# Decode attention: weights loaded first and used as moving operands, the first pair of chunks inside TensorE's loop, VectorE and ScalarE in rolled loops

## The chip, the cores and the metric

The kernel runs on one core of a Trainium2 chip. The metric is the device time of one execution in microseconds (us). The kernel before takes 665.26 us (median of 4 runs beside the changed kernel, 665.17 to 665.36). Profiles come from one execution each. They start at the first instruction, end about 2 us short of the measured time (663.3 of 665.2 us in the kernel before), and need not fall on the median run; where that matters, the text says so. All times inside an execution are counted from the span's start.

Names of engines: TensorE (PE in the profile; PEld is its weight load), VectorE (DVE), ScalarE (ACT), GpSimd (POOL), and the sync engine (SP), whose sequencer issues nearly all DMAs.

## The reference, cut to what matters

```python
x = A_x                                   # 1 x 1 x 512
xn = _layernorm(x)
# A: 32 query heads on 8 groups of cached keys and values, 65536 keys of 128 each
q = (xn @ wq)                             # 512 x 4096
scores = q k^T * 128 ** -0.5; p = softmax(scores); o = p v
a = o @ wo                                # 4096 x 512
# B: a small feed-forward block
h = gelu(xn @ w1 + b1)                    # 512 x 1792
b = h @ w2 + b2                           # 1792 x 512
return x + a + b
```

The keys and values are 2 x 134 MB, the weights 12 MB more. All must be read once; the arithmetic per byte is small.

## The kernel before

The cache is cut into 32 chunks of 16384 keys, four to a group: K0 to K31 and V0 to V31, 4 MB each. Two chunks make a pair. There are four 4 MB slots in SBUF: two for keys (0 and 1), two for values (2 and 3). At the start, wq lies in slot 2 and w1 with w2 in slot 3. The sync engine issues the chunks in one fixed order, each as soon as its slot is free:

```python
chunks = [("K", 0), ("K", 1)]
for u in range(2, NU):
    chunks += [("K", u), ("V", u - 2)]
...
after_chunk[("K", 0)] = [dma_small, dma_wq]     # x, biases; then wq
after_chunk[("K", 1)] = [dma_w12]
```

A pair transposes each key tile on TensorE (VectorE and ScalarE copy the transposes out of PSUM), multiplies them with q, takes the softmax's maximum and exponentials, and multiplies the values of the pair before. A key slot is free when all of its chunk is transposed (`done_chunk("K", ...)`), so K4 can be asked for only when K2 is transposed, in pair 1.

```python
def pair(i):
    ua, ub = 2 * i, 2 * i + 1
    first = i == 0
    ...
    transposes(0, 3)
    done_chunk("K", ua)
    if first:
        layernorm()
        qproj()              # 128 matmuls, wq stationary, one column each
        load_q(ua)
        scores(0, 0)
    ...
    scores(0, 3)
    v_block(ua - 2, 2)       # nothing when first
    v_block(ua - 2, 3)
    ...
    if first:
        ffn2()
    ...
```

Pair 0 stands in front of TensorE's loop, which then runs 15 turns for pairs 1 to 15. VectorE and ScalarE are unrolled altogether:

```python
@block.scalar
def _(e):
    _emit(e, ACT.ops)
@block.vector
def _(e):
    _emit(e, DVE.ops)
@block.tensor
def _(e):
    folded, growth = _fold([PE.ops[a:b] for a, b in zip(marks, marks[1:])])
    _emit(e, PE.ops[:marks[0]])               # pair 0
    _emit_loop(e, folded, growth, len(marks) - 1)
    _emit(e, PE.ops[marks[-1]:])
```

Of the kernel before, what the change touches and what calls it, by code (L numbers as in the profile page):

```python
# [22 lines left out]
class _Eng:  # L23
    def __init__(self, name, sem, is_pe=False):
        self.name = name
        self.sem = sem
        self.count = 0
        self.clock = {}
        self.ops = []
        self.is_pe = is_pe  # L30
        self.deferred = []

# [11 lines left out]
class _Sched:  # L44


    def __init__(self, nc):
        self.nc = nc
        self.engs = {}
        self.last_write = {}  # L50
        self.reads = {}
        self.dsem_vals = {}

# [52 lines left out]
    def op(self, eng, fn, reads=(), writes=(), publish=True, inc=1):  # L106
        req = self._required(reads, writes)
# [16 lines left out]
        eng.ops.append((waits, fn, pub))  # L124
        return ev

    def wait_ev(self, eng, ev):
        if not eng.knows(ev):
            eng.absorb(ev)
            eng.ops.append(([(ev.sem, ev.val)], None, None))  # L130

    def dma(self, eng, fn, sem, reads=(), writes=(), total=None):
# [14 lines left out]
        eng.ops.append((waits, fn, (sem, 16)))  # L147
# [3 lines left out]
def _fold(bodies):  # L151
# [5 lines left out]
    for i, b in enumerate(bodies):  # L157
        for k, (waits, _, _) in enumerate(b):
            for s, v in waits:
                seen.setdefault((k, s), {})[i] = v  # L160
# [5 lines left out]
    for k in range(len(bodies[0])):  # L166
        assert len({(b[k][2] or (None, 0))[1] for b in bodies}) == 1
        need = {}
        for (kk, s), at in seen.items():
            if kk == k:  # L170
                need[s] = max(v - i * growth[s] for i, v in at.items())
        ops.append((bodies[0][k][1], bodies[0][k][2], need))
    out = []
    known = {}
    for fn, pub, need in ops:
        waits = [(s, v) for s, v in need.items() if known.get(s) is None or known[s] < v]
        for s, v in waits:
            known[s] = v
        out.append((waits, fn, pub))
# [3 lines left out]
def _emit(eng_obj, ops):  # L183
    for waits, fn, pub in ops:
# [9 lines left out]
def _emit_loop(eng_obj, ops, growth, n):  # L194

    uses = {}
    for waits, _, _ in ops:
        for s, v in waits:
            uses.setdefault(s, []).append(v)
    regs, steps = {}, []  # L200
    at = {}
    for s, vs in uses.items():
        key = (vs[0], growth[s]) if len(vs) == 1 else s
        if key not in regs:
            r = eng_obj.alloc_register(f"w{len(regs)}")
            eng_obj.reg_mov(r, vs[0])
            regs[key] = r
            steps.append((r, vs[0] + growth[s] - vs[-1]))
        at[s] = [regs[key], vs[0]]
    with eng_obj.Fori(0, n):  # L210
        for waits, fn, pub in ops:
            for s, v in waits:
                r, now = at[s]
                if v != now:
                    eng_obj.reg_add(r, r, v - now)
                    at[s][1] = v
# [4 lines left out]
        for r, step in steps:  # L221
            eng_obj.reg_add(r, r, step)


def bass_parallel_sum__gqa_block_cached__dense_activation_gelu__decode_kernel(
# [74 lines left out]
    fin_bf = nc.alloc_sbuf_tensor("fin_bf", [128, 128], BF)  # L300

# [21 lines left out]
    negm = nc.alloc_sbuf_tensor("negm", [128, NU * HPG], F32)  # L323
    sums = nc.alloc_sbuf_tensor("sums", [128, NU * HPG], F32)
    o_all = nc.alloc_sbuf_tensor("o_all", [128, NU * HPG], F32)
    nmin = nc.alloc_sbuf_tensor("nmin", [128, H], F32)
    coef = nc.alloc_sbuf_tensor("coef", [128, NU * HPG], F32)
    wtot = nc.alloc_sbuf_tensor("wtot", [128, NU * HPG], F32)
    rden = nc.alloc_sbuf_tensor("rden", [128, H], F32)
    o_c = nc.alloc_sbuf_tensor("o_c", [128, NU * HPG], F32)  # L330
    o_sum = nc.alloc_sbuf_tensor("o_sum", [128, H], F32)
# [32 lines left out]
    for t, res in ((wo_cur, "wo_cur"), (oT_next, "oT_next"), (sums_cur, "sums_cur")):  # L364
# [15 lines left out]
    chunks = [("K", 0), ("K", 1)]  # L380
    for u in range(2, NU):
# [36 lines left out]
    def dma_small():  # L418
        for dst, src, res in (
# [5 lines left out]
            sch.dma(SP, lambda dst=dst, src=src: sp.dma_start(out=dst, in_=src), sem_misc,  # L425
# [33 lines left out]
    after_chunk[("K", 0)] = [dma_small, dma_wq]  # L459
    after_chunk[("K", 1)] = [dma_w12]  # L460
# [71 lines left out]

    def load_q(u):
        g = u // CPG
        sch.op(DVE, lambda g=g: dve.tensor_copy(out=q_cur[:, :], in_=qT_bf[:, g * HPG:(g + 1) * HPG]),
               reads=["qT"], writes=["q_cur"])
# [11 lines left out]
    def stats_2(u):  # L548
        k, us = u % 2, slice(u * HPG, (u + 1) * HPG)
# [5 lines left out]
               reads=["pA"], writes=[f"negm{u}"])  # L555
        src = pss[k][:, 0:CW].rearrange("p (t j) -> p t j", j=HPG)
        for j in range(HPG):
            sch.op(
                ACT,
                lambda k=k, u=u, j=j, src=src: act.activation(  # L560
                    out=P_v[k][:, :, j], in_=src[:, :, j], func=ACTF.Exp,
                    bias=negm[:, u * HPG + j:u * HPG + j + 1], scale=1.0,
                    accum_out=sums[:, u * HPG + j:u * HPG + j + 1]),
                reads=[f"negm{u}", f"pss{k}"],
                writes=[f"P{k}_{j}", f"sums{u}_{j}"],
# [15 lines left out]
    def keep_o(u):  # L581
        us = slice(u * HPG, (u + 1) * HPG)
        sch.op(DVE, lambda us=us: dve.tensor_copy(out=o_all[:, us], in_=pO[:, 0:HPG]),  # L583
               reads=["pO"], writes=[f"o{u}"])


    def qproj():
        for h in range(H):
            for kt in range(KT):
                sch.op(  # L590
                    PE,
                    lambda h=h, kt=kt: pe.matmul(  # L592
                        pA[:, PA_Q + h:PA_Q + h + 1], lhsT=wq_sb[:, kt, h * DH:(h + 1) * DH],
                        rhs=xnT_bf[:, kt:kt + 1], start=kt == 0, stop=kt == KT - 1),
                    reads=[f"slot{NK}", "xnT"], writes=["pA"],
                    publish=h == H - 1 and kt == KT - 1,
                )
        sch.op(DVE, lambda: dve.tensor_scalar(out=qT_bf[:, :], in0=pA[:, PA_Q:PA_Q + H], scalar1=SCALE,
                                              scalar2=None, op0=ALU.mult), reads=["pA"], writes=["qT"])
        slot_free[NK] = True  # L600

    def ffn1():
        for fc in range(FC):
            for kt in range(KT):
                sch.op(
                    PE,
                    lambda fc=fc, kt=kt: pe.matmul(  # L607
                        pA[:, PA_H + fc:PA_H + fc + 1], lhsT=w1_sb[:, kt, fc:F:FC],
                        rhs=xnT_bf[:, kt:kt + 1], start=kt == 0, stop=kt == KT - 1),
                    reads=[f"slot{NK + 1}", "w1", "xnT"], writes=["pA"],  # L610
                    publish=fc == FC - 1 and kt == KT - 1,
                )
# [15 lines left out]
    def ffn2():  # L628
        for kt in range(KT):
            cols = slice(kt * 128, (kt + 1) * 128)  # L630
            for fc in range(FC):
                sch.op(
                    PE,
                    lambda kt=kt, fc=fc, cols=cols: pe.matmul(  # L634
                        pA[:, PA_FT + kt:PA_FT + kt + 1], lhsT=w2_sb[:, fc, cols],
                        rhs=gT_bf[:, fc:fc + 1], start=fc == 0, stop=False),
                    reads=[f"slot{NK + 1}", "w2", "gT"], writes=["pA"], publish=False,
                )
            sch.op(
                PE,  # L640
                lambda kt=kt, cols=cols: pe.matmul(
                    pA[:, PA_FT + kt:PA_FT + kt + 1], lhsT=rows_bf[:, cols], rhs=ones2_bf[:, :],
                    start=False, stop=True),
                reads=["row0", "row1", "ones2"], writes=["pA"], publish=kt == KT - 1,
            )
        sch.op(DVE, lambda: dve.tensor_copy(out=finT[:, :], in_=pA[:, PA_FT:PA_FT + KT]),
               reads=["pA"], writes=["finT"])
# [7 lines left out]
    negm_v = negm[:, :].rearrange("p (g h j) -> p g h j", h=CPG, j=HPG)  # L655
    negm_r = negm[:, :].rearrange("p (g h j) -> p g j h", h=CPG, j=HPG)
    coef_v = coef[:, :].rearrange("p (g h j) -> p g h j", h=CPG, j=HPG)
    wtot_r = wtot[:, :].rearrange("p (g h j) -> p g j h", h=CPG, j=HPG)
    oc_r = o_c[:, :].rearrange("p (g h j) -> p g j h", h=CPG, j=HPG)
    GW = CPG * HPG  # L660

    def weigh_1(g):
        hs, cs = slice(g * HPG, (g + 1) * HPG), slice(g * GW, (g + 1) * GW)
        neg = [f"negm{u}" for u in range(g * CPG, (g + 1) * CPG)]
        sch.op(DVE, lambda: dve.tensor_reduce(out=nmin[:, hs], in_=negm_r[:, g], axis=AX.X, op=ALU.min),
               reads=neg, writes=[f"nmin{g}"])
        sch.op(DVE, lambda: dve.tensor_tensor(
            out=coef_v[:, g], in0=nmin[:, hs].unsqueeze(1).to_broadcast([128, CPG, HPG]), in1=negm_v[:, g],
            op=ALU.subtract), reads=[f"nmin{g}"] + neg, writes=[f"coef{g}"])
        sch.op(DVE, lambda: dve.tensor_copy(out=sums_cur[:, :], in_=sums[:, cs]),  # L670
               reads=[f"sums{u}_{j}" for u in range(g * CPG, (g + 1) * CPG) for j in range(HPG)],
               writes=["sums_cur"])
        sch.op(ACT, lambda: act.activation(out=coef[:, cs], in_=coef[:, cs], func=ACTF.Exp),
               reads=[f"coef{g}"], writes=[f"coef{g}"])
# [5 lines left out]
    def weigh_2(g):  # L680
# [228 lines left out]
```

## Time and profile before

| | before |
|---|---|
| time, median of 4 | 665.26 us |
| read from HBM | 280.5 MB |
| share of the data queue in 16 DMA engines' span | 99.1% |
| TensorE busy | 84% |
| K4 asked for at | 64.8 us |

The kernel is bound by its DMA stream. These are lines of its page: the rate in 40 equal slices, and the queues with packets, megabytes and the share of all 16 engines' span that their packets took.

```profile
GB/s 380 417 433 430 427 426 433 431 427 429 437 428 428 429 429 435 427 429 431 427 433 429 429 429 425 431 427 437 425 429 431 427 437 427 427 425 434 433 421 249
q1 hardware_dynamic: 14732, 280.51, 99.1%
q8 instruction: 14, 0.23, 0.1%
q14 instruction: 10, 0.08, 0.0%
```

Only the first two slices and the last are below 421 GB/s. The table by stretches has 429 GB/s from 100 to 200 us and 430 from 34 to 620. Queues q8 and q14 carry instructions, 24 packets in all.

A part of the table by stretches (busy time of each engine, then PE's granted clock, the DMA share and GB/s) looks like this:

```profile
70.00:80.00 10.00, 7.74 (x145) 7.21 (x141) 4.04 (x9) 2.05 (x2) 0.00 (x0) 0.61 1.00 426
80.00:90.00 10.00, 8.87 (x247) 8.52 (x245) 3.92 (x7) 5.41 (x12) 0.00 (x0) 0.91 1.00 425
90.00:100.00 10.00, 6.50 (x127) 5.79 (x124) 2.81 (x6) 1.02 (x1) 0.00 (x0) 0.50 1.00 426
```

The stream does not pause, because the next chunks are asked for in good time. The timeline of the sync engine shows when; K2, V0, K3, V1 and K4 are these issues:

```profile
22.14 0.33 SPq L412 DMA_DIRECT2D kv<-in_A_k_cache_dram  x1
28.77 0.33 SPq L412 DMA_DIRECT2D kv<-in_A_v_cache_dram  x1
46.14 0.33 SPq L412 DMA_DIRECT2D kv<-in_A_k_cache_dram  x1
54.23 0.33 SPq L412 DMA_DIRECT2D kv<-in_A_v_cache_dram  x1
64.84 0.33 SPq L412 DMA_DIRECT2D kv<-in_A_k_cache_dram  x1
```

TensorE is not free of trouble. In its timeline four starts in pair 1, its first turn of the loop, come after a wait for nothing that the profile shows ("issue", in the brackets: length of the wait and what ended it):

```profile
67.18 0.39 PE L574 MATMUL pO<-P_bf,kv 128*128 128x4 bf16 x10 [1.04 <-issue]
73.14 1.36 PE L574 MATMUL pO<-P_bf,kv 128*128 128x4 bf16 x45 [2.26 <-issue]
87.22 0.76 PE L574 MATMUL pO<-P_bf,kv 128*128 128x4 bf16 x24 [1.12 <-issue]
94.18 1.71 PE L574 MATMUL pO<-P_bf,kv 128*128 128x4 bf16 x58 [3.50 <-issue]
```

They sum to 7.9 us and cost nothing, because the queue is full meanwhile. By the DMA records each of the four ends 1.3 to 1.5 us after an instruction packet of 16 KB has arrived on q8. Later turns have no such waits, and from 99 to 653 us no packet on q8.

### The profile page before, as it was taken

Reading aid. Unit: us, or ns where it says so; the run is one execution under the profiler, and the core shown is the slowest. Engines: PE = TensorE matmul, PEld = TensorE weight load, DVE = VectorE, ACT = ScalarE, POOL = GpSimd, SP = SyncE. Lnnn points to the kernel's source line nnn. Section 1 sums busy time; section 2 is a strip of 40 time slices with the busy share of each in tenths; the row PEclk is TensorE's granted clock in tenths of the full one; section 3 lists DMA queues with packets and bytes.
Section 4 is the critical chain, followed back from the end, with each engine's and each line's share of the span. In section 5 each row is a group of like instructions: output and inputs, shape, how many; then the busy total and the mean of one; then the engine's idle time right before and its main releaser. Section 6 shows DMA issues by size and latency. Waiting matters only on the chain.

```text
span 663.3 us, 27482 instructions
## 1 busy us (share of the span) xinstructions
PE 560.4 (84%) x12846; PEld 529.3 (80%) x12846; DVE 274.0 (41%) x628; ACT 244.5 (37%) x469; POOL 2.3 (0%) x13
## 2 busy tenths in 40 slices
PE   1799879998887898888799888898888899778896
PEld 1689769898787888887788777888778898777895
DVE  0445324454443444443344443345433354433441
ACT  1354224444332344332344422344423344422340
POOL 1000000000000000000000000000000000000000
PEclk9887668887676788676788667888767888766885
DMA  9999999999999999999999999999999999999996
GB/s 380 417 433 430 427 426 433 431 427 429 437 428 428 429 429 435 427 429 431 427 433 429 429 429 425 431 427 437 425 429 431 427 437 427 427 425 434 433 421 249
DMA packets 14756, 280.82 MB, mean 423 GB/s; under 512 B 1674, under 2 KB 5772, under 8 KB 6028
## 3 DMA queue, kind: packets, MB, share of 16 engines
q1 hardware_dynamic: 14732, 280.51, 99.1%
q8 instruction: 14, 0.23, 0.1%
q14 instruction: 10, 0.08, 0.0%
HBM read 280.50 MB, written 0.00 MB: 423 GB/s over the span
## 4 chain that ended last, share of the span: by engine, by line
DMA 62%; PE 34%; issue 2%; ACT 1%; SPq 0%; DVE 0%
DMA kv<-in_A_k_cache_dram 57%; PE pst L499 25%; DMA wo_end<-in_A_wo_dram 5%; PE pss L519 4%; PE pO L574 2%; PE pA L540 1%; PE pA L550 1%; PE pA L592 1%; PE pA L607 1%; ACT kt_ring L509 0%; PE pA L634 0%; SPq L406 0%; ACT P_bf L560 0%; ACT L560 0%; ACT L484 0%
## 5 line engine op out<-in xcount | busy, mean ns | idle before, releaser
L499 PE MATMUL pst<-ident_bf,kv 128*128 128x128 bf16 x4096 | 315.8, 246 | 84.2 <-DMA kv<-in_A_k_cache_dram 82.6
L499 PEld LDWEIGHTS pst<-ident_bf,kv 128*128 128x128 bf16 x4096 | 287.3, 112 | 103.5 <-DMA kv<-in_A_k_cache_dram 71.4
L509 ACT ACTIVATE kt_ring<-pst 128x1024 bf16<-128x1024 bf16 x192 | 197.8, 1031 | 394.0 <-PE pst L499 391.3
L507 DVE COPY kt_ring<-pst 128x1024 bf16<-128x1024 bf16 x320 | 212.0, 688 | 216.7 <-PE pst L499 216.3
L574 PE MATMUL pO<-P_bf,kv 128*128 128x4 bf16 x4096 | 120.6, 165 | 10.0 <-issue 8.3
L519 PE MATMUL pss<-q_cur,kt_ring 128*128 128x4 bf16 x4096 | 121.3, 164 | 2.0 <-issue 1.5
L574 PEld LDWEIGHTS pO<-P_bf,kv 128*128 128x128 bf16 x4096 | 113.9, 100 | 11.2 <-issue 8.7
L519 PEld LDWEIGHTS pss<-q_cur,kt_ring 128*128 128x128 bf16 x4096 | 116.1, 97 | 2.2 <-issue 1.6
L527 DVE TENSOR_REDUCE pmax<-pss 128x4 f32<-128x512 f32 x32 | 22.1, 692 | 101.8 <-PE pss L519 101.8
L560 ACT ACTIVATE P_bf<-pss,negm 128x128 bf16<-128x128 f32 x128 | 50.8, 552 | 7.6 <-DVE negm L553 7.6
L560 ACT ACTIVATION_READ_ACCUMULATOR P_bf<-pss,negm 128x1 f32 x128 | 36.1, 282 | 0.0
L583 DVE COPY o_all<-pO 128x4 f32<-128x4 f32 x31 | 5.0, 162 | 38.3 <-PE pO L574 38.3
L540 PE MATMUL pA<-ident_f,pmax 128*4 128x128 f32 x64 | 16.9, 362 | 0.3 <-DVE finT L712 0.3
L550 PE MATMUL pA<-diag,ones_f 4*128 4x4 f32 x64 | 12.4, 261 | 0.3 <-DVE finT L712 0.3
L550 PEld LDWEIGHTS pA<-diag,ones_f 4*128 4x128 f32 x64 | 9.6, 186 | 3.6 <-DVE finT L712 0.3
L542 DVE TENSOR_REDUCE gmax<-pA 4x1 f32<-4x128 f32 x32 | 8.6, 269 | 0.7 <-PE pA L540 0.7
L540 PEld LDWEIGHTS pA<-ident_f,pmax 128*4 128x4 f32 x64 | 2.9, 84 | 6.0 <-DVE kt_ring L507 5.3
L544 DVE TENSOR_SCALAR diag<-ident_f,gmax 4x4 f32<-4x4 f32 x32 | 7.0, 217 | 1.1
L677 PE MATMUL pA<-sums_cur,ones_f 128*128 128x16 f32 x32 | 6.2, 270 | 0.0
L553 DVE TENSOR_SCALAR negm<-pA 128x4 f32<-128x4 f32 x32 | 5.1, 160 | 0.7 <-PE pA L550 0.7
L707 PE MATMUL pA<-oT_cur,wo_cur 128*128 128x1 bf16 x120 | 5.3, 165 | 0.0
L592 PE MATMUL pA<-xnT_bf,kv 128*128 128x1 bf16 x128 | 3.5, 164 | 1.8 <-DVE xnT_bf L487 1.8
(74 smaller groups left out, 62.2 us busy)
## 6 DMA issues: line engine op xcount, KB each, us to landing
kv<-in_A_k_cache_dram SPq DMA_DIRECT2D x32, 4096.0 KB, 28.4
kv<-in_A_v_cache_dram SPq DMA_DIRECT2D x31, 4096.0 KB, 32.3
kv<-in_A_wq_dram SPq DMA_DIRECT2D x1, 4096.0 KB, 20.1
kv<-in_B_w_dram SPq DMA_DIRECT2D x2, 1792.0 KB, 36.5
wo_cur<-in_A_wo_dram SPq DMA_DIRECT2D x13, 256.0 KB
kv<-in_A_v_cache_dram SPq DMA_DIRECT2D x1, 2048.0 KB, 27.5
kv<-in_A_v_cache_dram SPq DMA_DIRECT2D x1, 1024.0 KB, 29.6
kv<-in_A_v_cache_dram SPq DMA_DIRECT2D x2, 512.0 KB, 30.8
```

The lines of the kernel that those rows point to most:

```text
L499: lambda tb=tb, at=at, b=b, tt=s * TPB + t: pe.transpose(pst[tb][:, at * 128:(at + 1) * 128], slot[b][:, tt, :], ident_bf[:, :]),
L507: e, fn = DVE, lambda tb=tb, dst=dst: dve.tensor_copy(out=dst, in_=pst[tb][:, :])
L509: e, fn = ACT, lambda tb=tb, dst=dst: act.activation(out=dst, in_=pst[tb][:, :], func=ACTF.Copy)
L519: lambda k=k, kb=kb, at=at, t=t: pe.matmul(pss[k][:, at:at + HPG], lhsT=kt_ring[:, kb * BCOL + t * 128:kb * BCOL + (t + 1) * 128], rhs=q_c ...
L527: lambda k=k: dve.tensor_reduce(out=pmax[:, :], in_=pss[k][:, 0:CW].rearrange("p (t j) -> p j t", j=HPG), axis=AX.X, op=ALU.max),
L540: sch.op(PE, lambda: pe.matmul(pA[0:HPG, PA_ST:PA_ST + 128], lhsT=pmax[:, 0:HPG], rhs=ident_f[:, :], start=True, stop=True), reads=["pmax" ...
L542: sch.op(DVE, lambda: dve.tensor_reduce(out=gmax4[:, :], in_=pA[0:HPG, PA_ST:PA_ST + 128], axis=AX.X, op=ALU.max), reads=["pA"], writes=[" ...
L544: sch.op(DVE, lambda: dve.tensor_scalar(out=diag4[:, :], in0=ident_f[0:HPG, 0:HPG], scalar1=gmax4[0:HPG, 0:1], scalar2=None, op0=ALU.mult) ...
L550: sch.op(PE, lambda: pe.matmul(pA[:, PA_SB:PA_SB + HPG], lhsT=ones_f[0:HPG, 0:128], rhs=diag4[0:HPG, 0:HPG], start=True, stop=True), reads ...
L560: lambda k=k, u=u, j=j, src=src: act.activation(out=P_v[k][:, :, j], in_=src[:, :, j], func=ACTF.Exp, bias=negm[:, u * HPG + j:u * HPG + j ...
L574: lambda k=k, b=b, t=t: pe.matmul(pO[:, 0:HPG], lhsT=slot[b][:, t, :], rhs=P_v[k][:, t, :], start=t == 0, stop=t == TPD - 1),
L592: lambda h=h, kt=kt: pe.matmul(pA[:, PA_Q + h:PA_Q + h + 1], lhsT=wq_sb[:, kt, h * DH:(h + 1) * DH], rhs=xnT_bf[:, kt:kt + 1], start=kt == ...
```

## The change

The intent is a smaller program, with less instruction traffic, and projections that are out of the way before the keys arrive. It has four parts:

- wq, w1 and w2 are issued first; K0 and K1 after them. The projections run before pair 0, with the weights as moving operand (512 or 256 columns) and the vector as stationary one: 87 matmuls in place of 244, with the 12 that turn rows into columns.
- With the projections gone from pair 0, TensorE's loop holds it too: 16 turns. What pair 0 must not do (value products, statistics and output projection of a pair before) stands under guards, which the first turn jumps over.
- VectorE and ScalarE run loops of their own, a turn for each group from the second on; the first stands in front.
- x and the biases are loaded by ScalarE's queue.

```diff
@@ class _Sched
+    def part(self, skip):
+        self.guard, self.hole = True, skip
+        yield
+        self.guard, self.hole = False, False
@@ _emit_loop
+        for j, (guard, part) in enumerate(runs):
+            if guard:
+                with eng_obj.If_ne(later, 0):
+                    body(part, True)
+            else:
+                body(part, False)
+        if later is not None:
+            eng_obj.reg_mov(later, 1)
@@ order of the DMAs
-    chunks = [("K", 0), ("K", 1)]
-    for u in range(2, NU):
+    chunks = [("K", 0), ("K", 1), ("V", 0), ("K", 2), ("V", 1), ("K", 3)]
+    for u in range(4, NU):
         chunks += [("K", u), ("V", u - 2)]
-            sch.dma(SP, lambda dst=dst, src=src: sp.dma_start(out=dst, in_=src), sem_misc,
+            sch.dma(ACT, lambda dst=dst, src=src: act.dma_start(out=dst, in_=src), sem_misc,
-    after_chunk[("K", 0)] = [dma_small, dma_wq]
-    after_chunk[("K", 1)] = [dma_w12]
+    dma_small()
+    dma_wq()
+    dma_w12()
@@ qproj
-        for h in range(H):
+        for b in range(2):
             for kt in range(KT):
-                        pA[:, PA_Q + h:PA_Q + h + 1], lhsT=wq_sb[:, kt, h * DH:(h + 1) * DH],
-                        rhs=xnT_bf[:, kt:kt + 1], start=kt == 0, stop=kt == KT - 1),
+                for j in range(4):
+                    c0 = (b * 4 + j) * 512
+                    rows_mm(b, j, 512, xnT_bf[:, kt:kt + 1], wq_sb[:, kt, c0:c0 + 512], ...)
+        # then two evictions of 128x512 and 8 matmuls that turn the rows into columns
@@ pair
         def v_block(u, s):
-            if not first:
+            with sch.part(first):
                 pv(u, range(s * TPB, (s + 1) * TPB))
@@ emission
-            _emit(e, ACT.ops)
+            _emit_rolled(e, ACT.ops, [m[1] for m in marks2[1:]])
-            _emit(e, DVE.ops)
+            _emit_rolled(e, DVE.ops, [m[0] for m in marks2[1:]], 1, group)
-            _emit(e, PE.ops[:marks[0]])
-            _emit_loop(e, folded, growth, len(marks) - 1)
+            _emit_rolled(e, PE.ops, marks)
```

(Left out: ffn1 and ffn2 in the same moving form, smaller per-group tables of statistics so that a loop can use them, and four small matmuls that bring the feed-forward result into the output.)

## The prediction

> **What bounds the kernel now.** The DMA stream. The page counts 280.5 MB read in a span of 663.3 us; the queue table gives the data queue 99.1% of 16 engines' span. In the table by stretches the DMA share is 1.00 from 34 to 620 us, at 425 to 433 GB/s[...]. PE is busy 84%, but the wait table gives it 82.6 us of waiting for key chunks. DVE (41%) and ACT (37%) mostly wait for PE. A chunk takes 28 to 32 us from issue to landing, about 10 of them transfer, so two more are always queued. The stream loses time only at its ends: about 2.4 us before full rate (13.6 MB in the first 34 us, against 14.6 at 430 GB/s), about 3 us while the 16 engines finish unevenly (654 to 660 us), and 3.1 us of work and output after the last landing.
>
> **What the change does.** No byte of K, V or weights is saved.
> - Weights before keys: I estimate wq landing at 13 us, w1/w2 at 22, K0 at 31, K1 at 41 (bytes over 0.43 MB/us). The queue stays full if the first V chunk is issued by 39 us (it needs only the q projection) and K2 by 49 us.
> - Projections with weights moving: 32 matmuls of 512 columns in place of 128 of one. A 128-column transpose takes 59 ns at full clock, 107 at half, so I estimate 8 to 14 us for q (3.5 before), 3.4 to 6 for ffn1 (3.5), 3.6 to 6.5 for ffn2 (2.3). PE gets more work, but does it while K0 is arriving. Transposes of K0 start near 31 to 36 us and K2 is issued near 41 to 47, just in time.
> - Rolled loops and pair 0 inside: the queue table shows 0.31 MB of instructions; I expect about half, worth 0.3 us of DMA. Guards, register adds and branches cost PE perhaps 1 us a pair, inside its 5 us of waiting.
> - x and biases from ACT: 6.5 KB no longer queue behind K0; layernorm runs before wq lands. No weight on the end.
> - Four extra small f32 matmuls in the tail come before the last landing.
>
> On the critical path lies only the DMA stream, so the gain is a few tenths of a microsecond.
>
> **Predicted: 664.9 us, 80% range 663.5 to 668.0.** Faster by over 2%: 0.01; within 2%: 0.94; slower by over 2%: 0.05.
>
> **What would show it.** Right: data queue at 99%, about 430 GB/s in every stretch from 34 to 650 us; PE waiting for K already in the first pairs (before, only from about 107 us); fewer instruction packets; the last landing within 1 us of 660 us. Wrong: a stretch below 400 GB/s between 40 and 60 us (K2 late), or PE never waiting for K.
>
> **What would make it wrong.** Instruction fetch. Before, PE shows "issue" gaps of 1.0 to 3.5 us in the first turn of its loop, and pair 1 took 42 us, above the 39.6 us its data need; later turns show no such gaps. [...] the loop, about 1,610 instructions or 100 KB before, grows by guards and may no longer stay resident. Then each pair costs 42 us or more and the program ends near 690 to 700 us. DVE and ACT loops, refetched through a full DMA queue, could stall evictions likewise.

(664.9 us is the 665.3 us of the kernel before less a few tenths, 0.3 of them for instructions. 59 and 107 ns are 32 transposes in 1.89 us from 60.15 us on and in 3.44 us from 74.5 us on, at a granted clock of 1.00 and 0.50. The loop's 100 KB fit six packets of 16 KB on q8 between 64.7 and 98.0 us, when its first turn runs. The 1 us a pair for guards and branches was the author's guess, with no measurement behind it, and so was the risk that a longer loop would not stay resident.)

## The result, and the profile after

The changed kernel takes 673.24 us (median of 4 runs, 672.52 to 675.13). The ratio is 1.0124, 95% interval 1.0103 to 1.0146. A ratio here is the mean time of one kernel's runs over that of the other's of the same rounds, so it is not quite the ratio of the medians. The profiled run is the slowest of the four, 675.13 us.

The page's lines after the change, as before:

```profile
GB/s 366 444 432 422 305 218 437 436 432 431 428 430 426 434 422 436 430 426 434 422 436 422 434 428 428 434 426 432 423 433 434 426 432 428 428 436 427 430 428 292
q1 hardware_dynamic: 14440, 280.50, 97.7%
q8 instruction: 9, 0.15, 0.1%
q10 hardware_dynamic: 292, 0.01, 0.0%
q14 instruction: 4, 0.03, 0.0%
```

Instruction traffic fell from 0.31 to 0.18 MB as intended. But slices 5 and 6 have only 305 and 218 GB/s. The table by stretches finds the place:

```profile
70.00:80.00 10.00, 1.92 (x71) 1.75 (x67) 0.69 (x1) 0.44 (x1) 0.00 (x0) 0.68 1.03 418
80.00:90.00 10.00, 9.79 (x149) 9.02 (x150) 5.90 (x12) 5.85 (x13) 0.00 (x0) 0.80 0.03 9
90.00:100.00 10.00, 10.00 (x275) 10.00 (x273) 3.28 (x8) 2.63 (x3) 0.00 (x0) 0.71 0.84 334
```

From 80 to 90 us the DMA engines did nothing: 9 GB/s. In the trace's DMA records no data packet is in flight from 82.3 to 92.0 us, 9.7 us. Before, there is no pause of even 0.3 us. This is nearly the whole loss: the last data packet ends at 670.0 us in place of 660.0, and 3.3 us follow it in both kernels.

The sync engine's timeline says why. These are V0, K2, V1, K3, and then K4 (from narrower windows of the same view):

```profile
27.41 0.33 SPq L474 DMA_DIRECT2D kv<-in_A_v_cache_dram  x1
46.10 0.33 SPq L474 DMA_DIRECT2D kv<-in_A_k_cache_dram  x1
46.47 0.44 SPq L474 DMA_DIRECT2D kv<-in_A_v_cache_dram  x1
69.41 0.33 SPq L474 DMA_DIRECT2D kv<-in_A_k_cache_dram  x1
91.07 0.33 SPq L474 DMA_DIRECT2D kv<-in_A_k_cache_dram  x1
```

All that was asked for before K4 is 33.0 MB (wq, w1, w2 and six chunks). The stream starts at 1.8 us and has moved it by 82.3 us, which is 410 GB/s over that time. In the kernel before the same 33.0 MB stand ahead of K4, in another order, so its deadline lay at about the same place; it asked at 64.8 us, some 16 us early. The changed kernel asked 26 us later than that, at 91.1.

K4 waits for K2 to be transposed, so the delay is TensorE's. Its timeline has these lines (the first line is VectorE's first step of layernorm, from the timeline too):

```profile
19.65 0.17 DVE L529 CAST xT_f<-xT_bf 128x4 f32<-128x4 bf16 x1 [17.70 <-DMA rows_bf<-in_B_b_dram]
...
23.78 3.58 PE L657 MATMUL pss<-kv,xnT_bf 128*1 128x512 bf16 x32 [2.93 <-DVE xnT_bf L550]
...
37.95 5.53 PE L562 MATMUL pst<-ident_bf,kv 128*128 128x128 bf16 x96
...
50.30 1.59 PE L582 MATMUL pss<-q_cur,kt_ring 128*128 128x4 bf16 x49 [3.08 <-issue]
57.53 3.59 PE L562 MATMUL pst<-ident_bf,kv 128*128 128x128 bf16 x32 [5.63 <-issue]
...
72.18 1.74 PE L582 MATMUL pss<-q_cur,kt_ring 128*128 128x4 bf16 x63 [2.00 <-issue]
80.20 3.59 PE L562 MATMUL pst<-ident_bf,kv 128*128 128x128 bf16 x32 [6.28 <-issue]
```

Two things are seen. Layernorm starts only at 19.6 us, although wq (4 MB) landed at 13.1 us (12.4 us after its issue). It waits for all four small loads of 1 to 3.5 KB (x, b1, x once more as a row, b2), because they share one semaphore: by the DMA records the packets of x itself had ended at 12.8 us, and that of b2, the last, at 18.6, with its signal at 19.2. So the projections and pair 0 start late, pair 0 at 37.95 us. And pair 0 stands still four times, 17.0 us in sum, waiting for neither data nor an engine. The two long waits, 5.6 and 6.3 us, come directly after the longest guarded bodies, two value blocks (64 matmuls and their weight loads), and two value blocks with the output projection (72). Between 38 and 81 us the DMA records show seven instruction packets of 16 KB on q8, and each of the four waits ends 1.2 to 2.0 us after such a packet has arrived. That q8 carries TensorE's code is read from the runs: unrolling VectorE and ScalarE takes q14 from 4 packets to 10 and leaves q8 at 9 (e4), and putting pair 0 in front of TensorE's loop takes q8 from 9 to 13 and leaves q14 at 4 (e1).

So the theory is: **F**, TensorE ran pair 0 through code that it had not yet fetched; where a guard jumps over a body, the target was not there, and the fetch goes through the DMA engines that the stream keeps full (the queue table counts q8, as the data queue, in the 16 engines' span). Rivals: **X**, the late start alone is enough; **R**, the rolled loops of VectorE and ScalarE hold evictions back; **B/G**, guards, branches and register waits cost by themselves; and the moving form of the projections.

### The profile page after: what moved, and what is told of

Read it like the earlier page. It is cut to its first block, busy times and chain, and to the rows that moved or that the text cites. A ratio compares the mean times of both kernels' runs of the same rounds, so it can differ in the third digit from the quotient of the medians. Undisturbed runs are those within 1.5% of the kernel's fastest.

```text
span 673.3 us, 28125 instructions
## 1 busy us (share of the span) xinstructions
PE 559.5 (83%) x12701; PEld 521.2 (77%) x12701; DVE 276.7 (41%) x634; ACT 243.5 (36%) x462; POOL 2.3 (0%) x14
## 3 DMA queue, kind: packets, MB, share of 16 engines
q1 hardware_dynamic: 14440, 280.50, 97.7%
## 4 chain that ended last, share of the span: by engine, by line
DMA 57%; PE 38%; issue 3%; DVE 0%; ACT 0%; SPq 0%; ACTq 0%; DVEq 0%
DMA kv<-in_A_k_cache_dram 50%; PE pst L562 27%; PE pss L582 5%; DMA wo_end<-in_A_wo_dram 5%; DMA rows_bf<-in_B_b_dram 3%; PE pO L642 2%; PE pss L657 2%; PE pA L607 1%; PE pA L618 1%; SPq L468 0%; ACTq L487 0%; ACT L547 0%; PE pA L694 0%; PE pA L742 0%; PE pss L904 0%
## 5 line engine op out<-in xcount | busy, mean ns | idle before, releaser
L562 PE MATMUL pst<-ident_bf,kv 128*128 128x128 bf16 x4096 | 311.9, 244 | 77.4 <-DMA kv<-in_A_k_cache_dram 65.2
L562 PEld LDWEIGHTS pst<-ident_bf,kv 128*128 128x128 bf16 x4096 | 283.3, 111 | 97.2 <-DMA kv<-in_A_k_cache_dram 67.2
L618 PE MATMUL pA<-diag,ones_f 4*128 4x4 f32 x64 | 12.4, 261 | 0.3 <-DVE finT L773 0.3
L657 PE MATMUL pss<-kv,xnT_bf 128*1 128x512 bf16 (+1 forms) x60 | 5.6, 525 | 2.9 <-DVE xnT_bf L550 2.9
## 6 DMA issues: line engine op xcount, KB each, us to landing
kv<-in_A_wq_dram SPq DMA_DIRECT2D x1, 4096.0 KB, 12.4
kv<-in_A_v_cache_dram SPq DMA_DIRECT2D x1, 2048.0 KB, 27.6
```

The lines of the kernel that those rows point to most:

```text
L562: lambda tb=tb, at=at, b=b, tt=s * TPB + t: pe.transpose(pst[tb][:, at * 128:(at + 1) * 128], slot[b][:, tt, :], ident_bf[:, :]),
L618: sch.op(PE, lambda: pe.matmul(pA[:, PA_SB:PA_SB + HPG], lhsT=ones_f[0:HPG, 0:128], rhs=diag4[0:HPG, 0:HPG], start=True, stop=True), reads ...
L657: sch.op(PE, lambda: pe.matmul(pss[b][32 * j:32 * j + 1, 0:n], lhsT=lhsT, rhs=rhs, start=k == 0, stop=last), reads=reads, writes=[f"pss{b} ...
```

## The experiments

Each of these kernels was correct. "Pair 0 waits" is the sum of TensorE's "issue" waits from the first transpose of K0 to the first of K2; "hole" is the time without any data packet; both, and the time K4 was asked for, belong to the profiled run, whose time is in the second column.

| run | profiled run, us | pair 0 waits, us | K4 asked for, us | hole, us | median, us | ratio to before (95%) |
|---|---|---|---|---|---|---|
| before | 665.2 | | 64.8 | none | 665.26 | 1 |
| after | 675.1 | 17.0 | 91.1 | 9.7 | 673.24 | 1.0124 (1.0103 to 1.0146) |
| e1_peel | 664.9 | 2.8 | 75.3 | none | 665.20 | 1.0004 (0.9987 to 1.0020) |
| e2_x_on_sync | 667.5 | 15.3 | 83.2 | 3.0 | 667.12 | 1.0021 (1.0004 to 1.0038) |
| e3_both | 666.5 | 2.9 | 74.0 | none | 663.92 | 0.9976 (0.9960 to 0.9993) |
| e4_unrolled | 674.6 | 13.7 | 87.7 | 7.6 | 674.60 | 1.0139 (1.0122 to 1.0156) |
| e5_old_projections | 670.0 | 13.3 | 85.4 | 5.1 | 670.55 | 1.0079 (1.0062 to 1.0096) |
| e6_dead_code | 672.6 | 14.4 | 85.9 | 5.4 | 675.64 | 1.0161 (1.0145 to 1.0178) |
| e7_dead_branches | 666.8 | 3.7 | 77.5 | none | 666.45 | 1.0009 (0.9992 to 1.0025) |
| e8_before_x_on_scalar | 665.6 | | 72.4 | none | 665.52 | 1.0001 (0.9985 to 1.0018) |
| e9_x_late | 682.6 | 13.4 | 98.4 | 7.0 and 7.8 | 681.83 | 1.0240 (1.0225 to 1.0256) |
| e10_both_again | 664.0 | 3.6 | 72.8 | none | 663.99 | 0.9979 (0.9966 to 0.9993) |
| e11_both_old_proj | 663.7 | 1.5 | 73.5 | none | 663.95 | 0.9990 (0.9976 to 1.0003) |

Read the columns of K4 and of the hole together, leaving out e9: up to 77.5 us there is no hole; from 83.2 us on the hole is K4's time less 80.1 to 81.3 us, in five kernels. That is a deadline, measured.

The hole is not all that separates the runs. In the profiled runs of e3, e6 and e7 the stream moved 402, 393 and 393 GB/s from 100 to 130 us, against 431 in the kernel after and 432 in e10. By these rates that is another 2 to 3 us each (an estimate), about what sets the profiled run of e3 above that of e10, which is the same kernel. Why the stream slows there is not shown. And the profiled run of the kernel after was its slowest, so its 17.0 and 9.7 us are on the high side.

### e1_peel: pair 0 in front of the loop again

```diff
-        self.guard, self.hole = True, skip
+        self.guard, self.hole = False, skip
...
-            _emit_rolled(e, PE.ops, marks)
+            _emit_rolled(e, PE.ops, marks[1:])
```

> Only edit to the kernel after: pair 0 of TensorE stands in front of the loop again, without guards; the loop runs 15 turns. Theory F (the DMA hole of 9.7 us at 82 us comes from TensorE running pair 0 through cold, guarded loop code, where its four long waits for nothing but code, 3.1, 5.6, 2.0 and 6.3 us, make it release key slot 0 late): those gaps shrink to below 4 us in sum in pair 0, K4 is issued before 80 us in place of 91.4, the hole goes, and the time is 663 to 666 us. Theory X (the late start of pair 0, 37.9 us in place of 13.3, is enough by itself): the hole stays near 10 us, 671 to 675 us.

Measured: 665.20 us, no hole, K4 at 75.3 us. Waits of TensorE in pair 0 of the kernel after, and below it of e1, from the tables of waits of these stretches (us in total, times, longest):

```profile
PE pst L562 <- issue: 11.9, 2, 6.3
...
PE pss L582 <- issue: 5.1, 2, 3.1
```

```profile
PE pst L562 <- issue: 1.7, 2, 1.4
...
PE pss L582 <- issue: 1.1, 1, 1.1
```

The 17.0 us became 2.8, and K4 came 15.8 us earlier. Theory X alone falls: pair 0 started at 36.9 us, hardly earlier than in the kernel after (37.95), and the hole is gone.

### e2_x_on_sync: x and the biases behind wq on the sync queue

```diff
-            sch.dma(ACT, lambda dst=dst, src=src: act.dma_start(out=dst, in_=src), sem_misc,
+            sch.dma(SP, lambda dst=dst, src=src: sp.dma_start(out=dst, in_=src), sem_misc,
...
-    dma_small()
     dma_wq()
+    dma_small()
     dma_w12()
```

> Only edit to the kernel after: x and the biases go back to the sync queue, behind wq. x should land with wq near 13 us in place of 19.4, and pair 0 should start near 31 us in place of 37.9. Theory X: with 6 us less lateness the hole shrinks by as much, 667 to 669 us, or goes if pair 0 started early enough. Theory F: pair 0 is paced by code fetch, whose gaps stay near 17 us in sum; the start moves them all forward, so again 667 to 670 us. If ScalarE's queue had nothing to do with it: 673 us.

Measured: 667.12 us. The four small loads had landed at 13.7 us in place of 19.6, pair 0 started at 33.1 in place of 37.95, K4 came 7.9 us earlier, and the hole shrank to 3.0 us. The waits in pair 0 stayed (15.3 us). So the late loads were worth about 6 of the 8 us lost (by the medians). Taking away the guards removed all of the loss (e1), taking away the late loads most of it: both consume time ahead of one deadline, so their shares do not add up. A semaphore for x alone might have done as much on ScalarE's queue, since x itself was through at 12.8 us; no run tried it.

### e3_both and e10_both_again: both edits

> Both edits together. Theory F and X alike: no hole, 663 to 665 us; K4 issued with more than 10 us of queue left. If it comes out above 666 us, a third cause exists.

> The kernel of e3_both again, unchanged, for a firmer comparison with the kernel before: 663.9 us in most runs, some at 666.5; ratio 0.997 to 0.999. No hole in the stream.

Measured: 663.92 us, one run of four at 666.47 (the profiled one); again with five rounds 663.99 us, 663.58 to 664.36. This version beats both kernels, by 0.2% against the one before (ratio 0.9979, interval 0.9966 to 0.9993), which is real but far below the 2% that a verdict asks for. In e10 the stream runs through:

```profile
70.00:80.00 10.00, 8.45 (x271) 8.15 (x268) 2.98 (x7) 3.28 (x7) 0.00 (x0) 0.77 0.98 416
80.00:90.00 10.00, 8.18 (x118) 7.68 (x118) 4.81 (x11) 3.92 (x8) 0.00 (x0) 0.71 1.00 424
90.00:100.00 10.00, 8.14 (x261) 7.84 (x259) 3.15 (x5) 3.54 (x7) 0.00 (x0) 0.80 1.00 424
```

Its last data packet ends at 658.9 us, 1.1 us before that of the kernel before. The 0.07 MB of instructions saved would be about 0.2 us at 430 GB/s, an estimate; where the rest comes from was not isolated.

### e4_unrolled: VectorE and ScalarE without loops

```diff
-            _emit_rolled(e, ACT.ops, [m[1] for m in marks2[1:]])
+            _emit(e, ACT.ops)
...
-            _emit_rolled(e, DVE.ops, [m[0] for m in marks2[1:]], 1, group)
+            _emit(e, DVE.ops)
```

> Only edit to the kernel after: VectorE and ScalarE run unrolled again (constant waits, no loops). Theories F and X: these engines follow TensorE in the hole, so 672 to 675 us, with the hole in place. Rival R (the rolled loops of VectorE and ScalarE hold back evictions by refetching code or by stricter waits): the hole shrinks by over 3 us and the time falls below 670 us.

Measured: 674.60 us, a hole of 7.6 us, the same four waits (13.7 us). Rival R falls: the rolled loops of these engines did not cause the loss, and neither saved time.

### e6_dead_code and e7_dead_branches: the disputed cost by itself

Both start from e1, where pair 0 stands outside the loop. The bodies that pair 0 skips are put back into TensorE's program between its parts, under branches on a register that holds zero, so they are never executed. In e7 each body is cut to its first matmul.

```diff
             if eng.is_pe:
-                eng.ops.append(([], None, None, True))
+                eng.ops.append(([], fn, None, "dead"))
...
+        if held:                               # in _emit: a run of dead operations
...
+            with eng_obj.If_ne(zero, 0):
+                for f in held:                 # e7: held[:1]
+                    f()
+            held = []
```

> e1_peel plus dead code: pair 0 stands in front of the loop, but the bodies that the guards skipped (value products, statistics, output projection) stay in TensorE's program between its parts, each jumped over by a branch that is always taken. The loop and its waits are those of e1. Theory F (what costs is jumping over code that then has to be fetched through a full DMA queue): the two gaps of about 6 us come back at the two longest jumps, K4 is issued near 88 to 91 us, the hole is 7 to 10 us, the time 671 to 675 us. Rival G (the loop's register waits, or guards as such): as e1, 665 us.

> As e6_dead_code, but each jumped-over body is cut to its first matmul: the same eight branches, hardly any dead code. Theory F: as e1_peel, 664 to 666 us, K4 issued near 76 us, no hole. Rival B (a taken branch costs microseconds by itself): as e6, above 670 us.

Measured: e6 took 675.64 us (its profiled run, 672.64, was its fastest), e7 666.45 us, half a microsecond above what was expected of it. The tables of waits for pair 0, with the value products of pair 1 left out; first e6, then e7:

```profile
PE pst L574 <- issue: 10.2, 2, 5.1
...
PE pss L594 <- issue: 4.2, 2, 2.2
```

```profile
PE pss L594 <- issue: 3.3, 2, 1.9
...
PE pst L574 <- issue: 0.4, 1, 0.4
```

With the dead code the four waits are back at the same four places (48.0, 54.5, 68.5 and 75.1 us), and so is the loss. With as many branches but hardly any dead code they are not. Rivals B and G fall: with eight taken branches the waits are 3.7 us, against 2.8 in e1, and the loop's register waits are those of e1 in both. The DMA records show the fetch itself: up to K2's first transpose six packets start on q8 in e6, as in the kernel after, and four in e7, as in e1, for the same executed work. So the code that was jumped over was fetched nevertheless, with packets starting 5.9 to 8.7 us apart in e6 and 6.2 to 9.7 in e7, while the work that would have covered the fetch was left out. The skipped bodies are small: two packets more for 256 value matmuls with their weight loads make the longest body (72) a little over half a packet, an estimate. Whether a body of several packets would be fetched too is not shown.

### e5_old_projections: weights stationary again

The edit puts back `qproj`, `ffn1` and `ffn2` of the kernel before, in the order of the kernel after, and drops the four matmuls that added the feed-forward row at the end.

> Only edit to the kernel after: the three projections have the weights as stationary operand again, as in the kernel before (244 one-column matmuls in place of 88, so about 310 more instructions). By the durations of before (3.5, 3.5 and 2.3 us) the projections alone would end some 2 to 3 us earlier than 38.0 us; but the extra code is fetched cold. Theory that the moving form delayed pair 0: hole shrinks by 2 to 3 us, 670 to 672 us. Theory F says the added cold code takes it back or more: 673 us or longer.

Measured: 670.55 us, pair 0 at 35.0 us in place of 37.95, a hole of 5.1 us. The moving form did delay pair 0 by 3 us, and the time fell by 2.7 us. That fits, but the waits in pair 0 came out shorter too (13.3 in place of 17.0 us), so it is not shown that the earlier start alone did it. The q projection itself was no slower (3.58 us in both forms); the time went to the evictions and turns around it, and to ffn2, 5.0 us in place of 2.3. That more code would take it back (expected from theory F) was wrong.

### e8_before_x_on_scalar: the ScalarE loads in the kernel before

```diff
-            sch.dma(SP, lambda dst=dst, src=src: sp.dma_start(out=dst, in_=src), sem_misc,
+            sch.dma(ACT, lambda dst=dst, src=src: act.dma_start(out=dst, in_=src), sem_misc,
```

> Only edit to the kernel before: x and the biases are loaded by ScalarE, in the same place of its program. x should land near 19 us here too[...] in place of about 13 us, but layernorm starts only after the transposes of K0, at 22.5 us, so the time stays at 665.3 us within 0.5 us. If it gets slower by over 1 us, the small loads hurt the stream itself.

Measured: 665.52 us, no difference. But the four loads together landed later than expected (x itself was through at 12.8 us here too), which the first step of layernorm shows:

```profile
27.56 0.17 DVE L466 CAST xT_f<-xT_bf 128x4 f32<-128x4 bf16 x1 [4.50 <-DMA rows_bf<-in_B_b_dram]
```

Layernorm moved from 22.5 to 27.6 us, and K4 from 64.8 to 72.4 us. The time did not notice, since the deadline is near 81. The edit cost margin and no time; in the kernel after, with the margin gone, e2 shows the like edit costing 6 us.

### e9_x_late: more lateness on purpose

```diff
-    dma_small()
     dma_wq()
     dma_w12()
+    after_chunk[("K", 0)] = [dma_small]        # and issued by the sync engine
```

> Only edit to the kernel after: x and the biases on the sync queue again, but behind the weights and K0, so that x lands near 31 us in place of 19.4. This makes the lateness of pair 0 larger on purpose. Theory (the hole is the sum of all delays of TensorE before K4 is asked for, less a margin that is used up): pair 0 starts about 12 us later than in the kernel after, near 50 us, K4 is issued near 103 us, and the time is 683 to 687 us. If the start of pair 0 did not matter one for one, below 678 us.

Measured: 681.83 us, a little under the expected band, and with two holes. Pair 0 started at 50.6 us. K2 itself was now late (58.7 us), so the stream ran dry there first, and again before K4 (98.4 us). The two lines are of the table by stretches:

```profile
50.00:60.00 10.00, 10.00 (x223) 9.52 (x222) 7.20 (x14) 6.07 (x6) 0.00 (x0) 1.00 0.24 82
90.00:100.00 10.00, 10.00 (x213) 9.38 (x212) 6.49 (x15) 7.23 (x14) 0.00 (x0) 0.96 0.19 57
```

A start 12.6 us later moved K4 by only 7.3 us. Part of the difference is that the first of pair 0's four waits (3.1 us) does not occur: the second code packet of pair 0 starts at 56.8 us, inside the first hole and 6.8 us after the one before it; in the kernel after, beside the full stream, it was 10.0 us. That fits theory F, but no run isolated it.

### e11_both_old_proj: e3 with the old projections

> e3_both with the projections in their old form. TensorE starts pair 0 up to 3 us earlier, but K0 lands near 31 us and K4 already had some 5 us of margin; theory: no gain from a start that is not needed, 663.5 to 666 us, the same as e10 within 1 us. If it is faster by over 1 us, the stream still loses time to TensorE.

Measured: 663.95 us, against 663.99 of e10 in the same rounds. That was expected, but not for this reason: pair 0 did not start earlier. The projections ended some 3 us earlier, and TensorE then waited for K0. The first transposes of e11, and below them those of e10:

```profile
32.72 7.25 PE L562 MATMUL pst<-ident_bf,kv 128*128 128x128 bf16 x96 [3.33 <-DMA kv<-in_A_k_cache_dram]
```

```profile
32.79 5.53 PE L562 MATMUL pst<-ident_bf,kv 128*128 128x128 bf16 x96 [0.73 <-DMA kv<-in_A_k_cache_dram]
```

So with the small loads on time the form of the projections made no difference: the landing of K0 set the start of pair 0. Whether an earlier start would buy anything was not tested.

## Why the prediction was wrong

The prediction was 664.9 us with a range of 663.5 to 668.0; 673.24 us was measured. The class was right (within 2%), the direction and the range were not. Point by point:

- **The bound: right.** The DMA stream bounds the kernel (its queue has 99.1% of the engines' span before, 97.7% after, the hole included), nothing of the bytes was saved, and no version here goes below 663.58 us in any run. The tail after the last data packet is 3.3 us in both kernels.
- **The deadline: the step that failed.** The prediction checked the queue for V0 (27.4 us, estimated limit 39) and for K2 (46.1 us, predicted 41 to 47, limit 49), found it "just in time", and stopped there. The failing transfer was K4, three requests further. Its limit is about 81 us; it was asked for at 91.1. The prediction called the stream the only thing on the critical path, but the change without its guards and ScalarE loads had already moved K4 from 64.8 us to the 72.8 of e10, half of the old margin of 16 us, and what was left had to cover the two errors below.
- **"Guards, register adds and branches cost PE perhaps 1 us a pair": a guess, and wrong, 17.0 us of waits in the first pair.** The prediction did name instruction fetch as the risk, but with the wrong mechanism: a loop that no longer stays resident and fetches in every turn. It stayed resident: after seven packets of 16 KB from 38 to 81 us, in the first turn, the trace has only two more TensorE code packets, both in the tail (663.9 and 668.9 us). The cost fell in the first turn alone. That it is the code jumped over, and not the guards, was shown by e1, e6 and e7.
- **"x and biases from ACT: layernorm runs before wq lands": wrong.** Layernorm began at 19.6 us, wq had landed at 13.1. On a queue of their own the small packets did not overtake the stream. The DMA records show the 128 packets of x, 8 bytes each, in groups of 16, one group every 1.2 us, beside data packets of 32 KB that take about as long; x was through at 12.8 us, about when wq was, and layernorm, waiting on the semaphore of all four loads, had to wait for the biases too. What sets that pace is not shown. e2 measured the cost: 6 us.
- **Projections: sizes off, outcome mostly harmless.** q was put at 8 to 14 us and took 3.58; ffn1 at 3.4 to 6 and took 2.04; ffn2 at 3.6 to 6.5 and took 5.0. The estimate multiplied single matmuls, but q and ffn1 write to four groups of output rows, and the trace shows four 512-column matmuls of q in 0.43 us, the time of one of the first of ffn2 (33.4 to 35.5 us). With evictions and turns the new form still started pair 0 some 3 us later (against e5).
- **"PE waiting for K already in the first pairs": wrong.** The first wait of TensorE for keys in the loop is at 182 us, later than before (131.7 us; the prediction had put that at 107).
- **Instructions: right.** 0.18 MB in place of 0.31; its worth, a few tenths, could not be seen behind the hole.
- **The last landing within 1 us of 660: wrong**, 670.0 us by the data packets, nearly all of it by the hole of 9.7 us.

What stays open: why each fetch comes so late. In the kernel after, the next code packet starts 3.6 to 5.0 us after TensorE resumes from a wait while the stream is full, and 0.6 us after it at 80.2 us, when the stream was running dry. That speaks for the full DMA engines as the cause, as e9 does, but these are two cases; no run fetched cold code beside an idle stream on purpose. It also stays open where e10's gain of 1.3 us comes from beyond the instructions saved.

## What to carry to other kernels

In a kernel bound by its DMA stream, an engine off the critical path still has deadlines (here TensorE's, for K4, near 81 us): write down, for every transfer until the steady state and not only for the first, when the bytes asked for before it run out and when its slot comes free, and treat each edit as spending that margin. The skipped code here, in bodies of little more than half a packet at most, was fetched all the same, so a guarded first turn of a large loop can be slower than the unguarded copy of it that it was meant to save (17.0 us of waits in pair 0, against 2.8 in e1); peel the odd turn off when, as here, its code is not yet fetched and the stream fills the DMA engines. And do not count on a second queue to bring small loads ahead of a large stream: here the four landed at 19.6 us on a queue of their own, and at 13.7 us behind the first transfer they are needed with (e2). Ask also which of them the first step really needs, because one semaphore for all makes it wait for the last (x was through at 12.8 us, layernorm began at 19.6).
